# An RWKV-7 and Fourier-mixing kernel: who makes the decay totals, who turns r and v, and a new instruction order

**Chip, cores, metric.** One core of one Trainium2 chip. The time is the device time of one execution in microseconds (us); medians of several executions are given, with lowest and highest. A ratio is the mean time of one kernel's runs over the mean of the other kernel's runs in the same rounds, with a 95% interval, so it is not quite the ratio of the medians quoted beside it. Chips differ by one or two us, so kernels of different rounds are compared by their ratios to the kernel before.

## The reference

Inputs r, k, v, w, a, b have the shape 4 x 8 x 768 x 40 (batch, heads, time, head size), in float32.

```python
for t in range(S):                                   # RWKV-7 recurrence, per batch and head
    y[:, :, t] = einsum('bhd,bhde->bhe', rt, state)
    Sa = einsum('bhde,bhe->bhd', state, at)
    state = state * wt[:, :, None, :] - einsum('bhd,bhe->bhde', Sa, bt) + einsum('bhd,bhe->bhde', vt, kt)
x = y.transpose(0, 2, 1, 3).reshape(B, S, 320)
mixed = real(fft(fft(x, axis=1), axis=2))            # Fourier mixing over time and features
u = x + mixed
un = (u - mean(u)) / sqrt(var(u) + 1e-6)
out = u + maximum(un @ w_ch1, 0) @ w_ch2             # w_ch1 320 x 1280, w_ch2 1280 x 320
```

## The kernel before

The recurrence is computed in 24 chunks of 128 time steps, 6 to a batch. Each chunk is prepared (six loads of 160 KB, logarithms and cumulative sums of w, scaled and transposed inputs), then its chain updates the state, and after a batch's last chunk come the Fourier mixing and the feed-forward part (`post`). All engines run fixed lists: `ORDER` gives, for every operation, its place and its engine, and `SLOTS` the buffer that each intermediate takes. Every engine works through its list in order. `WARM` entries are matmuls on zeros that do nothing but fill TensorE's time.

The state update of a chunk needs the product of all its decays (the "total", `wt`). It is made in one of two ways:

```python
last, by_pe = c == NCH - 1, c < NCH - 1 and i not in WT_DMA
...
if by_pe:                                   # nine small matmuls in sums(), then one exponential
    op({"ACT": ... wt = exp(cum[:, DM:DM + 2 * NP])}, w=[wt], r=[cum], kind="wt")
...
if not last and not by_pe:                  # the last row of the sums, then a DMA that spreads it over partitions
    wt, row = buf(wt_s), new_row()          # the row pool has two buffers
    op({"ACT": ... row[96:] = exp(cum[96:, :DM]) ...}, w=[row], r=[cum], kind="row")
    op({"SP": (0.49, lambda: nc.sync.dma_start(
        wt().rearrange("p e q -> p (e q)"), row()[C - 1:C, :8 * C].rearrange("o (p j) -> o p j", j=8)))},
       w=[wt], r=[row], dma=0.2, kind="total")
```

The loads go by the same queue, SyncE's (`SP`), each as one `nc.sync.dma_start`. r and v are transposed either by one DMA transpose on that queue (`i in TURN_RV`) or by eight TensorE transposes and two evictions. The second weight matrix is loaded by `W2_PARTS` DMAs from GpSimd's queue.

## Time and profile before

| kernel before | |
|---|---|
| median of 4 runs beside the changed kernel | 234.84 us (233.29 to 235.43) |
| span of the profiled run, mean granted clock | 231.9 us, 1.00 |
| loads that landed before 46 us: median time from landing to first use | 0.4 us (of 44 loads; middle half 0.1 to 0.8) |
| last load of the first batch lands / that batch's last chunk ends its chain | 43.9 / 53.5 us |

How to read it: a median of 0.4 us between landing and first use says that the first 46 us are paced by the loads, whatever the engines do. From 72.6 us on TensorE paces it (the prediction shows the chain). Two rows of the page, in 40 slices of 5.8 us, the granted TensorE clock and the busy share of the DMA engines in tenths:

```profile
PEclk9999999999999999999999999999999999999999
DMA  6999999989998999969498999998974440000213
```

The first row has no dip; the second is at eight or nine up to slice 29 (168 us), but for slices 1, 18 and 20.

### The profile page before, as it was taken

The numbers are of one execution on the slowest core, as the hardware profiler recorded it, in microseconds if no ns is written. First come the engines' busy times: TensorE is split into PE (matmuls) and PEld (weight loads), VectorE is DVE, ScalarE is ACT, GpSimd is POOL, SyncE is SP. The second block draws the span as 40 slices with busy tenths as digits, with TensorE's granted clock in tenths as the row PEclk, the third lists the DMA queues.
The fourth block names the chain that finished last, engine by engine and source line by source line (L and its number), as shares of the span: only waits on it lengthen the run. The fifth ranks groups of instructions, "written<-read, shape, count | busy, mean of one in ns | idle before, by whom it ended". The sixth has DMA issues, their size and how long they took to land.

```text
span 231.9 us, 8953 instructions
## 1 busy us (share of the span) xinstructions
PE 223.8 (96%) x3617; PEld 171.0 (74%) x3617; DVE 206.0 (89%) x399; ACT 188.7 (81%) x381; POOL 153.9 (66%) x241
## 2 busy tenths in 40 slices
PE   7989999999999999999999999999999999999994
PEld 2557777878877777788877778878777777776573
DVE  6999999999999999889898988998999989589563
ACT  8999998989999998669999978998999886345300
POOL 7388978989998998442979968748965844200000
PEclk9999999999999999999999999999999999999999
DMA  6999999989998999969498999998974440000213
GB/s 120 189 159 190 167 159 161 173 140 176 159 196 153 164 189 178 170 130 162 88 218 149 182 158 176 169 170 130 230 137 76 83 105 31 3 0 0 88 57 113
DMA packets 165400, 31.88 MB, mean 137 GB/s; under 512 B 160560, under 2 KB 165040, under 8 KB 165360
## 3 DMA queue, kind: packets, MB, share of 16 engines
q1 hardware_dynamic: 163680, 29.69, 72.7%
q0 software_dynamic: 1680, 1.64, 4.6%
q8 instruction: 28, 0.46, 0.8%
q14 instruction: 12, 0.10, 0.1%
HBM read 26.87 MB, written 3.93 MB: 133 GB/s over the span
## 4 chain that ended last, share of the span: by engine, by line
PE 71%; DVE 10%; DMA 8%; POOL 4%; issue 3%; SPq 2%; ACT 2%; POOLq 0%; ACTq 0%; DVEq 0%
PE ps L167 71%; DMA in<-in_k_dram 4%; DVE pr L167 3%; POOL nat L167 2%; DMA in<-in_a_dram 2%; SPq L167 2%; DMA in<-in_w_dram 2%; DVE xb L167 2%; DVE m L167 1%; DVE xs L167 1%; DVE kb L167 1%; POOL pr L167 1%; ACT rw L167 1%; DVE sm L167 1%; DVE ar L167 0%
## 5 line engine op out<-in xcount | busy, mean ns | idle before, releaser
L167 PE MATMUL ps<-unT,w1sb 128*128 128x384 bf16 x240 | 46.7, 326 | 0.0
L167 POOL TENSOR_SCALAR_AFFINE_SELECT pr<-pr 128x1024 bf16<-128x1024 bf16 x32 | 34.8, 1096 | 16.3 <-ACT pr L167 16.3
L167 POOL TENSOR_TENSOR nat<-in,rw 128x320 bf16<-128x320 f32 x42 | 36.1, 866 | 7.7 <-DMA in<-in_k_dram 4.9
L167 PEld LDWEIGHTS <-nat 128*128 128x128 bf16 x576 | 34.0, 97 | 9.4 <-POOL nat L167 2.5
L167 PE MATMUL ps<-ident,nat 128*128 128x128 bf16 x416 | 36.3, 219 | 1.8 <-POOL nat L167 1.0
L167 ACT ACTIVATE pr<-ps 128x1024 bf16<-128x1024 f32 x33 | 33.6, 1032 | 3.4 <-PE ps L167 3.1
L167 PE MATMUL ps<-w2sb,h 128*128 128x320 bf16 (+1 forms) x250 | 35.7, 294 | 0.0
L167 PEld LDWEIGHTS <-pr 128*128 128x128 bf16 x768 | 28.9, 96 | 6.6 <-DVE pr L167 0.6
L167 ACT ACTIVATE h<-ps 128x384 bf16<-128x384 f32 x48 | 23.0, 494 | 8.3 <-PE ps L167 8.1
L167 PEld LDWEIGHTS <-h 128*128 128x128 bf16 x250 | 23.1, 98 | 8.2
L167 DVE TENSOR_TENSOR pr<-ps,su 128x1024 bf16<-128x1024 f32 x23 | 27.9, 1217 | 0.8 <-PE ps L167 0.4
L167 PEld LDWEIGHTS <-w1sb 128*128 128x128 bf16 x240 | 21.0, 97 | 10.2
L167 POOL TENSOR_TENSOR pm<-xb 128x161 bf16<-128x161 f32 x39 | 20.0, 527 | 8.2 <-DVE xb L167 8.0
L167 POOL TENSOR_TENSOR nat<-in,wp 128x320 bf16<-128x320 f32 x22 | 19.2, 874 | 4.4 <-ACT wp L167 1.7
L167 DVE TENSOR_TENSOR m<-ps,su 128x1024 bf16<-128x1024 f32 x15 | 18.3, 1217 | 1.9 <-PE ps L167 1.5
L167 DVE TENSOR_TENSOR pr<-ps,nsu 128x1024 bf16<-128x1024 f32 x16 | 19.4, 1213 | 0.6 <-PE ps L167 0.6
L167 DVE TENSOR_SCALAR h<-ps 128x384 bf16<-128x384 f32 x32 | 16.5, 548 | 3.4 <-PE ps L167 3.3
L167 DVE SCALAR_TENSOR_TENSOR xb<-ps,bst,xb 128x320 f32<-128x320 f32 (+1 forms) x25 | 13.0, 531 | 5.1 <-PE ps L167 5.0
L167 PE MATMUL ps<-xs,pr 128*128 128x40 bf16 x384 | 17.3, 180 | 0.3 <-DVE xs L167 0.2
L167 PE MATMUL ps<-nat,pr 128*128 128x40 bf16 x384 | 17.2, 180 | 0.2 <-DVE pr L167 0.2
L167 PE MATMUL ps<-ar,kb 64*128 64x128 bf16 x384 | 16.7, 217 | 0.3 <-DVE pr L167 0.2
L167 POOL TENSOR_TENSOR low<-logw 128x320 f16<-128x320 f32 x19 | 13.7, 722 | 2.0 <-ACT logw L167 1.5
(145 smaller groups left out, 554.3 us busy)
## 6 DMA issues: line engine op xcount, KB each, us to landing
in<-in_w_dram SPq DMA_DIRECT2D x24, 160.0 KB, 3.7
in<-in_r_dram SPq DMA_DIRECT2D x24, 160.0 KB, 3.7
in<-in_a_dram SPq DMA_DIRECT2D x24, 160.0 KB, 3.8
in<-in_v_dram SPq DMA_DIRECT2D x24, 160.0 KB, 3.9
in<-in_b_dram SPq DMA_DIRECT2D x24, 160.0 KB, 3.9
in<-in_k_dram SPq DMA_DIRECT2D x24, 160.0 KB, 4.1
out_dram<-xb SPq DMA_DIRECT2D x23, 160.0 KB, 1.9
w2sb<-in_moe_w_ch_dram POOLq DMA_DIRECT2D x2, 400.0 KB, 6.3
```

Source lines behind the costliest of these rows:

```text
L167: i = f(*args, **kwargs)
```

## The change

The intent: less small work for TensorE early (totals of chunks 3, 4, 6 and 7 by DMA), fewer DMA transposes in the middle (r and v of chunks 16, 17 and 18 back on TensorE), the second weights in smaller pieces, and an order and buffer assignment made anew for this.

```diff
-TURN_RV = {16, 17, 18, 19, 20, 21, 22, 23}
+TURN_RV = {19, 20, 21, 22, 23}
-WT_DMA = {8, 9, 10, 11, 12, 13, 14, 15, 16, 17, 18, 19, 20, 21, 22, 23}
+WT_DMA = {3, 4, 5, 6, 7, 8, 9, 10, 11, 12, 13, 14, 15, 16, 17, 18, 19, 20, 21, 22, 23}
-W2_PARTS = 2
+W2_PARTS = 5
-ORDER = ("AJAAHDALDAIAAUDAPDAEDATD ... (some 2,200 entries)
+ORDER = ("AHAAIDCGGAdSATGBASAJAAQG ... (some 2,200 entries, all new; 38 filling matmuls for 24)
-SLOTS = ("BCADABBCAABCBAB ...
+SLOTS = ("ABCDABCABABCABA ...
```

## The prediction

> **What bounds the kernel now.** I read the page first, then the chain of waits, then a table of stretches, then the timelines of TensorE and of SyncE's DMA queue. The chain tells which engine sets the end, and when that begins:
>
> ```profile
> PE 71%; DVE 10%; DMA 8%; POOL 4%; issue 3%; SPq 2%; ACT 2%; POOLq 0%; ACTq 0%; DVEq 0%
> ...
> 29.00 3.67 DMA in<-in_w_dram
> 32.66 4.68 DMA in<-in_a_dram
> ...
> 43.73 5.47 DMA in<-in_k_dram
> ...
> 72.64 26.55 PE ps L167 x427
> ...
> 101.33 59.34 PE ps L167 x989
> ...
> 163.04 65.82 PE ps L167 x867
> ```
>
> The columns are start, length and what. Up to about 50 us the chain goes through input loads (three pieces of 3.7 to 5.5 us are shown), from 50 to 72 us through VectorE, and from 72.6 us to the end almost only through TensorE: 26.55 + 59.34 + 65.82 = 151.7 of the last 159 us. So time taken from TensorE after 72 us is worth its full length, and time taken from it before 50 us is worth little, because there it waits for loads. The stretches say the same (busy us and count of each engine, granted clock, DMA share, GB/s):
>
> ```profile
> 0.00:24.00 24.00, 21.12 (x299) 13.13 (x300) 21.30 (x42) 22.92 (x50) 17.10 (x52) 1.00 0.99 165
> 24.00:48.00 24.00, 22.83 (x483) 18.32 (x480) 22.96 (x35) 22.33 (x48) 20.91 (x31) 1.00 0.95 163
> 72.00:120.00 48.00, 47.83 (x753) 37.01 (x752) 44.52 (x95) 41.97 (x83) 36.38 (x50) 1.00 0.89 157
> 120.00:168.00 48.00, 47.88 (x835) 38.04 (x828) 44.25 (x82) 43.29 (x87) 37.55 (x53) 1.00 1.06 173
> ```
>
> VectorE and ScalarE are at 90% or more beside TensorE, and the DMA share is about 1 until 168 us. The clock is 1.00 everywhere. A busy TensorE is not a full one, so I worked out from the starts of all 3617 matmuls in the trace how much room there is: 197.6 us of work at each form's own spacing, 4.6 us of filling matmuls that do nothing, and 25.2 us of gaps. 16.8 us of the gaps are before 72 us and 8.4 us after it, 5% of that part. The prices of what the change moves come from TensorE's timeline where chunk 7's totals are made:
>
> ```profile
> 42.61 0.16 PE L167 MATMUL ps<-ones,logw 128*128 128x2 bf16 x1
> 42.63 0.16 PE L167 MATMUL ps<-ones,low 128*128 128x2 bf16 x1
> ...
> 42.81 0.17 PE L167 MATMUL ps<-off_d,ident 128*128 128x8 bf16 x1
> 42.84 0.30 PE L167 MATMUL ps<-logw,ut 128*128 128x320 bf16 x1
> 42.97 0.30 PE L167 MATMUL ps<-low,ut 128*128 128x320 f16 x1
> 43.11 0.39 PE L167 MATMUL ps<-ident,nat 128*128 128x128 bf16 x4
> 43.33 0.31 PE L167 MATMUL ps<-sn,nat 128*128 128x80 bf16 x4
> ```
>
> Read the starts, not the lengths: the nine small matmuls of one total take 42.84 - 42.61 = 0.23 us, although each is shown as 0.16 us long; a group of four transposes takes 43.33 - 43.11 = 0.22 us.
>
> **What the Trainium skill says.** "TensorE: Matmul & The Clock Gate", section "Wait — 56ns, not 53.3ns?", gives the warm spacing as N / 2.4 GHz plus about 2.5 ns, and a floor of about 25 ns however small N is. The trace agrees: 55 ns for each transpose of 128 columns, 25 to 26 ns for each matmul of 2 columns. "Perfetto Trace Analysis", section "Tensor Engine Instruction (MATMUL, LD_WEIGHTS)", says that matmul ends are estimated; this is why I take starts. "DMA: Bandwidth & Descriptors", section "Anatomy of one DMA — SWDGE (gpsimd) path", says that a DMA's semaphore wait is held by the issuing sequencer before dispatch, so an early total whose row isn't ready would hold up the loads behind it. The trace has a mild form: SyncE's queue waited 2.2 us for ScalarE's rows in two places. The same page, "Specifications", gives 512 B as the least size for line rate; here 160560 of 165400 packets are smaller, and the loads bring 163 to 173 GB/s at a full share.
>
> **The change part by part.**
>
> *Totals.* A total is made by DMA from chunk 3 on instead of chunk 8; chunk 5 is the last of its batch and has none, so four chunks change (3, 4, 6, 7). TensorE loses 4 x 9 matmuls, 4 x 0.23 = 0.92 us. ScalarE loses 4 x 0.18 us (wt) and gains 4 x 0.43 us (row): +1.0 us. The queue gains four DMAs of 4 KB. These chunks are prepared between about 18 and 59 us, mostly where TensorE waits for loads anyway, so I count a good third of the 0.92: -0.35 us.
>
> *r and v.* Chunks 16, 17 and 18 go back to TensorE: 3 x 8 = 24 transposes, 6 groups of 0.22 = +1.33 us, between about 120 and 152 us, in the middle of the 59 us piece of the chain, so all of it counts. VectorE or ScalarE gets three more evictions of 512 columns (0.42 us on VectorE, 0.60 on ScalarE) and three that are 1024 wide instead of 512 (about +0.4 us each): some 2.6 us on two engines that have 8.5 us free between them from 120 to 168 us. It fits, with less slack. Three DMA transposes leave the queue (1.3 us to issue, 3.3 us to landing each). From 120 to 168 us the DMA is full, but TensorE has only some 3 us of gaps there, so I give that relief -0.3 us.
>
> *Second weights.* Two DMAs of 400 KB, 0.94 us each on GpSimd, become five of 160 KB, by the 0.66 us of a first-weight DMA about 3.3 us: +1.4 us on GpSimd, which is idle 34% of the span. They were issued at 80 and 82 us and first used after 94 us. Hidden: 0.
>
> *Order.* In the built order the last load of the first batch is DMA 38 of SyncE's queue (one of the 37 before it a total) and was DMA 42. At the measured pitch, 42 issues from 0.8 to 39.7 us or 0.95 us each, the batch is complete 3.8 us earlier, and the second half's work, which keeps TensorE full, can begin earlier. The price: chunks 6, 7 and 8 are complete 2, 4 and 5 places later (46 for 44, 53 for 49, 62 for 57). From 36 to 60 us the gaps were 4.9 of 24 us, 20%; 3.8 us of such time turned full is worth 0.2 x 3.8 = -0.8 us. The engine choices move too: counting forms in both built orders at the durations of the table of forms, VectorE loses about 1.5 us, ScalarE is even within 0.2, GpSimd gains about 6 us (six more folds, three more low parts, five weight DMAs). Slack goes to the engines that lack it; I give it -0.7 us of the 8.4 us of late gaps. The filling matmuls rise from 10,824 to 16,472 columns, 4.5 to 6.9 us at 2.4 GHz, all but a little in the first 25 us or so, where TensorE waits: 0, with a risk of half a microsecond.
>
> The sum: -0.35 + 1.33 - 0.3 - 0.8 - 0.7 = -0.8 us, so 234.6 - 0.8 = 233.8. The new order was presumably made for these settings and kept because it was good, so I take a little more off: **233.2 us**.
>
> **The rivals.**
> 1. *The late transposes decide.* TensorE is the bound from 120 to 168 us, the order's gains are small, and the time rises by the 1.33 us and some waits for the added evictions: 235.5 to 236.5. For it: the chain has nothing but TensorE there, with VectorE at 92%. Against it: the same order moves work off VectorE.
> 2. *Early totals become a wait.* When the DMA is full a total lands late: the eighth's was issued at 63.3 and landed at 69.7 us, and the state update that needs it began at 72.0. Chunk 4's total is now DMA 43; it would be issued at about 41 us, land at about 47, and chunk 4's update ran at 44.2 us before, so the state could come some 2.5 us late, and everything of chunk 5 behind it in TensorE's fixed order. If nothing else fills, this takes the 0.8 us back and costs 1 to 2 more: 235 to 237. Against it: the new order may have room just there, and a total isn't always so slow (median 2.6 us).
> 3. *The early part gains more.* The gaps before 72 us are 16.8 us, and loads at 38 instead of 42 may close 3 to 4 us of them, as TensorE is full once the first batch is complete: 230 to 231. Against it: no load has become cheaper, what comes earlier for one chunk comes later for the next, and the later chunks had only 0.6 to 3 us of slack.
>
> | step | effect on the end, us |
> |---|---|
> | totals | -0.35 |
> | r and v on TensorE | +1.33 |
> | DMA relief from 120 to 168 us | -0.3 |
> | weights in five | 0 |
> | first batch earlier | -0.8 |
> | later gaps | -0.7 |
>
> **Range and chances.** The 2% line is 4.7 us, at 229.9 and 239.3. The named terms are all under 1.4 us; only the order could move more, and it has 25 us of gaps to work on, of which I don't expect over 4 to go. The runs of before spread over 2.1 us. Eight times in ten I expect 229.8 to 236.4. Faster by over 2%: 0.11; within 2%: 0.84; slower by over 2%: 0.05.
>
> **What would show it.** Right: TensorE's matmuls on row totals fall from 28 + 28 + 7 to 12 + 12 + 3 and transposes of nat rise from 416 to 440; the chain goes into TensorE's long pieces a few us before 72.6; between 120 and 168 us TensorE stays as full as before with 24 more transposes. Rival 1 would show as more gaps of TensorE on VectorE and ScalarE evictions from 120 to 168 us. Rival 2 would show as a state update of chunk 3, 4, 6 or 7 that starts on a landing, "DMA wt<-row" in the chain. Rival 3 would show as 3 us or more fewer gaps before 72 us. I'm wrong in kind if the last load of a later batch, or a weight transfer, appears in the chain after 72 us.

## The result, and the profile after

| | before | changed |
|---|---|---|
| median (lowest to highest), 4 runs each | 234.84 us (233.29 to 235.43) | 240.61 us (240.19 to 241.99) |
| ratio | | 1.0266 (1.0201 to 1.0331): slower |
| span and clock of the profiled run | 231.9 us, 1.00 | 239.0 us, 0.993 |
| clock in the four runs | 1.00 in the profiled run | 0.993, 0.993, 0.993, 0.986 |
| median time from landing to first use, loads up to 46 us | 0.4 us | 2.3 us |
| last load of the first batch lands / its last chain ends | 43.9 / 53.5 us | 37.8 / 53.6 us |

Executions over 1.5% slower than the fastest of the same kernel are left out of the means. The prediction (233.2 us, 229.8 to 236.4) is wrong: the time lies 4.2 us above the range. The page of the changed kernel:

```profile
PEclk9999999999997999999999999999999999999999
DMA  7999998969999899989372798889478520002104
...
PE 73%; ACT 11%; DVE 6%; DMA 4%; issue 3%; POOL 2%; ACTq 0%; DVEq 0%; POOLq 0%
PE ps L168 73%; DMA wt<-row 4%; ACT pr L168 2%; DVE pr L168 1%; ACT h L168 1%; ACT wp L168 1%; ACT row L168 1%; POOL nat L168 1%; ACT logw L168 1%; DVE h L168 1%; ACT nat L168 1%; ACT kb L168 1%; ACT rw L168 1%; DVE xs L168 1%; POOL sm L168 1%
```

The share of input loads in the chain has gone (there were 8% of DMA, nearly all loads), and one other transfer has come: `wt<-row`, a total, with 4%. The clock has a dip in slice 13 (72 to 78 us). The chain of waits of the changed kernel, as start, length and what:

```profile
61.73 8.53 DMA wt<-row
70.82 0.95 PE ps L168 x19
72.31 10.79 PE ps L168 x175
...
86.25 33.64 PE ps L168 x509
119.91 23.93 PE ps L168 x426
```

and its waits from 58 to 98 us (engine, what it wrote, what it waited for: us, times, longest):

```profile
ACT row L168 <- DMA wt<-row: 3.1, 1, 3.1
PE ps L168 <- ACT row L168: 2.6, 1, 2.6
```

Which total? The one issued at 61.73 us is chunk 8's, which both kernels make by DMA. It takes 8.5 us to land. Chunk 10's row has the same of the two row buffers and waits for that, ScalarE waits with it, and TensorE waits for the PSUM bank that the row is read from. TensorE stands for 2.8 us from 68.0 us on, and from 72.61 to 76.02 us its clock is granted at 0.5. Stretches of both kernels (busy us and count of TensorE, its weight loads, VectorE, ScalarE and GpSimd, then granted clock, DMA share, GB/s), first before, then changed:

```profile
48.00:60.00 12.00, 11.53 (x242) 9.64 (x239) 11.59 (x16) 10.79 (x25) 11.07 (x18) 1.00 0.95 162
60.00:72.00 12.00, 11.77 (x225) 9.64 (x221) 11.86 (x28) 11.95 (x23) 11.20 (x18) 1.00 1.06 180
```

```profile
48.00:60.00 12.00, 11.94 (x242) 10.11 (x240) 11.89 (x19) 11.83 (x26) 11.85 (x17) 1.00 0.81 137
60.00:72.00 12.00, 9.16 (x163) 7.37 (x161) 9.18 (x22) 8.87 (x19) 8.74 (x13) 1.00 1.03 178
72.00:84.00 12.00, 11.90 (x195) 9.17 (x194) 10.80 (x25) 11.36 (x25) 10.28 (x16) 0.86 0.93 155
```

TensorE, VectorE, ScalarE and GpSimd fall to about 9 of 12 us between 60 and 72 us, while the DMA is full again; and just before, from 48 to 60 us, the DMA was at 0.81. So transfers that could have been made before 60 us were made after it. Why, the experiments have to say.

Busy time hides how full TensorE is, so I worked out real work, filling matmuls and gaps from the starts of all matmuls (each at its form's own spacing, the rest of the distance to the next start being gap, so what half clock costs is counted as gap; us):

| stretch | before: work, fill, gap | changed: work, fill, gap |
|---|---|---|
| 0 to 36 | 20.4, 4.4, 9.9 | 17.9, 6.5, 10.4 |
| 36 to 60 | 18.9, 0.1, 4.9 | 19.7, 0.3, 3.9 |
| 60 to 96 | 32.6, 0.0, 3.4 | 28.6, 0.2, 7.2 |
| 96 to 192 | 89.8, 0.0, 6.2 | 89.8, 0.0, 6.2 |
| 192 to the end | 35.8, 0.0, 0.8 | 42.1, 0.0, 1.5 |

The late middle, where 24 transposes came in, is exactly as full as before. 4.0 of the 6.3 us of work that the changed kernel still has to do after 192 us were lost between 60 and 96 us.

### The profile page after: what moved, and what is told of

It reads as the page before. It is cut to its first block, busy times and chain, and to the rows that moved or that the text cites.

```text
span 239.0 us, 8965 instructions
## 1 busy us (share of the span) xinstructions
PE 228.5 (96%) x3619; PEld 175.2 (73%) x3619; DVE 204.9 (86%) x398; ACT 189.2 (79%) x379; POOL 158.8 (66%) x249
## 4 chain that ended last, share of the span: by engine, by line
PE 73%; ACT 11%; DVE 6%; DMA 4%; issue 3%; POOL 2%; ACTq 0%; DVEq 0%; POOLq 0%
PE ps L168 73%; DMA wt<-row 4%; ACT pr L168 2%; DVE pr L168 1%; ACT h L168 1%; ACT wp L168 1%; ACT row L168 1%; POOL nat L168 1%; ACT logw L168 1%; DVE h L168 1%; ACT nat L168 1%; ACT kb L168 1%; ACT rw L168 1%; DVE xs L168 1%; POOL sm L168 1%
## 5 line engine op out<-in xcount | busy, mean ns | idle before, releaser
L168 PE MATMUL ps<-unT,w1sb 128*128 128x384 bf16 x240 | 47.2, 326 | 0.0
L168 POOL TENSOR_SCALAR_AFFINE_SELECT pr<-pr 128x1024 bf16<-128x1024 bf16 x31 | 33.7, 1093 | 16.7 <-ACT pr L168 16.5
L168 POOL TENSOR_TENSOR nat<-in,rw 128x320 bf16<-128x320 f32 x44 | 38.0, 871 | 4.9 <-ACT nat L168 2.8
L168 PEld LDWEIGHTS <-nat 128*128 128x128 bf16 x600 | 34.9, 98 | 8.1 <-POOL nat L168 1.8
L168 PE MATMUL ps<-ident,nat 128*128 128x128 bf16 x440 | 36.6, 219 | 1.0 <-ACT nat L168 0.3
L168 PEld LDWEIGHTS <-pr 128*128 128x128 bf16 x768 | 29.3, 96 | 8.4 <-issue 2.9
L168 PE MATMUL ps<-w2sb,h 128*128 128x320 bf16 (+1 forms) x250 | 35.2, 294 | 0.0
L168 ACT ACTIVATE pr<-ps 128x1024 bf16<-128x1024 f32 x32 | 32.5, 1024 | 1.3 <-PE ps L168 0.9
L168 DVE TENSOR_TENSOR pr<-ps,su 128x1024 bf16<-128x1024 f32 x25 | 30.3, 1219 | 2.2 <-PE ps L168 1.1
L168 ACT ACTIVATE h<-ps 128x384 bf16<-128x384 f32 x54 | 25.3, 495 | 5.4 <-PE ps L168 5.2
L168 PEld LDWEIGHTS <-h 128*128 128x128 bf16 x250 | 23.3, 98 | 8.4
L168 PEld LDWEIGHTS <-w1sb 128*128 128x128 bf16 x240 | 20.4, 97 | 10.4 <-DVE unT L168 0.2
L168 POOL TENSOR_TENSOR pm<-xb 128x161 bf16<-128x161 f32 x45 | 22.1, 509 | 6.6 <-DVE xb L168 6.5
L168 POOL TENSOR_TENSOR nat<-in,wp 128x320 bf16<-128x320 f32 x22 | 19.0, 865 | 3.3 <-ACT wp L168 2.3
L168 PE MATMUL ps<-nat,pr 128*128 128x40 bf16 x384 | 17.0, 180 | 2.6 <-ACT row L168 2.6
L168 DVE TENSOR_TENSOR pr<-ps,nsu 128x1024 bf16<-128x1024 f32 x15 | 18.2, 1216 | 1.3 <-PE ps L168 1.2
L168 DVE TENSOR_TENSOR m<-ps,su 128x1024 bf16<-128x1024 f32 x15 | 18.2, 1216 | 0.9 <-ACT h L168 0.8
L168 DVE SCALAR_TENSOR_TENSOR xb<-ps,bst,xb 128x320 f32<-128x320 f32 (+1 forms) x25 | 12.7, 530 | 7.1 <-PE ps L168 6.8
L168 POOL TENSOR_TENSOR low<-logw 128x320 f16<-128x320 f32 x22 | 15.8, 720 | 4.2 <-ACT logw L168 4.2
L168 PE MATMUL ps<-ar,kb 64*128 64x128 bf16 x384 | 17.9, 221 | 0.4
L168 PE MATMUL ps<-xs,pr 128*128 128x40 bf16 x384 | 17.3, 180 | 0.2
L168 DVE TENSOR_SCALAR h<-ps 128x384 bf16<-128x384 f32 x26 | 13.8, 547 | 2.3 <-PE ps L168 1.9
```

The costliest lines, as they stand in the source:

```text
L168: i = f(*args, **kwargs)
```

## The experiments

All are timed against the kernel before in the same rounds. All outputs are correct except where said.

Two tools serve throughout. Where two kernels have the same order, I pair the same matmuls of their traces and compare the starts; "behind" and "ahead" mean this. And each timed run has its mean clock: a stretch of 3.41 us at half clock in a span of 239 us makes 0.993, so the clock tells which of the timed runs had one.

| run | median us (before in its rounds) | ratio (95%) |
|---|---|---|
| changed kernel | 240.61 (234.84) | 1.0266 (1.0201 to 1.0331) |
| new_order_old_settings | 249.33 (235.85) | 1.0562 (1.0532 to 1.0592) |
| old_order_new_settings | 249.59 (235.85) | 1.0590 (1.0545 to 1.0635) |
| own_row_for_chunk_10 | 243.17 (235.85) | 1.0335 (1.0279 to 1.0391) |
| first_weights_after_total | 242.30 (235.85) | 1.0282 (1.0255 to 1.0309) |
| early_totals_on_tensore | 238.04 (234.46) | 1.0116 (1.0054 to 1.0179) |
| early_totals_on_scalar_queue | 241.54 (234.46) | 1.0278 (1.0216 to 1.0341) |
| all_totals_on_scalar_queue | 253.81 (234.46) | 1.0789 (1.0701 to 1.0876) |
| old_order_early_totals_only | 246.52 (234.46) | 1.0495 (1.0419 to 1.0571) |
| four_idle_transfers | 240.75 (235.30) | 1.0247 (1.0175 to 1.0318) |
| total_of_7_three_loads_later | 239.05 (235.30) | 1.0107 (1.0003 to 1.0211) |
| old_order_early_totals_later | 237.38 (235.30) | 1.0131 (1.0034 to 1.0229) |
| old_order_rv_on_tensore | 240.78 (235.30) | 1.0245 (1.0163 to 1.0327) |
| no_late_fills | 237.55 (235.44) | 1.0081 (1.0054 to 1.0108) |
| early_totals_on_gpsimd_queue | 242.80 (235.44) | 1.0314 (1.0281 to 1.0348) |
| twelve_fills_in_old_order | 237.97 (235.44) | 1.0117 (1.0089 to 1.0145) |
| old_order_totals_from_10 | 235.33 (235.44) | 0.9986 (0.9965 to 1.0008) |
| early_totals_on_tensore_again | 240.18 (237.63) | 1.0144 (1.0086 to 1.0202) |
| r_v_not_turned (wrong result) | 238.70 (237.63) | 1.0048 (1.0025 to 1.0070) |

### First round: order against settings, and the two things at 61 us

My first theory was that the order is to blame, and that the settings are worth their few tenths. The first run takes the new order with the three old settings, the second the old order with the new ones; what a setting adds or drops was placed by hand.

```diff
 # new_order_old_settings: new ORDER,       # old_order_new_settings: old ORDER,
-WT_DMA = {3 ...}; TURN_RV = {19 ...}       -WT_DMA = {8 ...}; TURN_RV = {16 ...}
+WT_DMA = {8 ...}; TURN_RV = {16 ...}       +WT_DMA = {3 ...}; TURN_RV = {19 ...}
```

> The new order with all three settings of before (totals on TensorE for chunks 3, 4, 6, 7; r and v of chunks 16 to 18 turned by DMA; second weights in two). Theory A (the order costs the time: a row of chunk 10 that waits for a total in flight at 67 to 70 us, and a slow start): it stays slow, 238 to 241 us, since chunk 8's total and chunk 10's row are there with either setting. Rival B (the three settings cost the time): back to 233 to 236 us.

> The old order with all three settings of after, each added or dropped operation put at the place of the one that it replaces (one more buffer for turned a and r; the index table shares the second weights' memory). Theory A: within 2 us of before, 233.5 to 237 us, by the sum of the prediction's small terms and some for the unplanned places. Rival B: 239 us or more.

Both lie near 249.5 us, outside what either theory said. They don't tell order from settings, as each breaks the fit of one to the other. The first loses its time from 120 to 168 us, where its hand-placed DMA transposes of r and v land late: its chain has `157.97 5.21 DMA rv<-nat` there. But from 60 to 96 us it does 32.1 us of TensorE work, nearly the 32.6 of before and far from the 28.6 of the changed kernel, in the same order. So in this trace the loss at 60 us is missing although the order is the new one, which hints at a setting. That was the first useful hint; the fifth round shows its limit. The second run loses its time before 60 us, and is taken up below.

The next two take on the chain's own account: the row buffer, and the three transfers of the first weights issued between 59.8 and 61.9 us.

```diff
 # own_row_for_chunk_10
-row = new_row()
+row = buf(h1_s, ...) if i == 10 else new_row()      # a buffer that is free then, zeroed on GpSimd
 # first_weights_after_total: in ORDER, on GpSimd
-weights 1, 2, 3 at 59.8, 61.3 and 61.9 us
+weights 1, 2, 3 after chunk 9's second cast (67 us)
```

> After, with a row buffer of its own for chunk 10's total (in a tile of h that is free then), so that its row need not wait for chunk 8's total to be read. Theory A: the 3.1 us wait of ScalarE at 67 us is gone, TensorE's gap of 2.6 us and the stretch at half clock after it too: 3 to 4.5 us faster than after, 236 to 237.5 us. Rival B: less than 1 us of difference.

> After, with the three first-weight DMAs issued some us later on GpSimd, so that chunk 8's total is in the queues before them. If crowding by those weights makes the total take 8.5 us (theory A1), it lands in 2.5 to 5 us, the wait of ScalarE shrinks to 0 to 1 us and the time falls by 2 to 4 us, to 236.5 to 238.5 us, unless the weights now come late for the first use. If the loads ahead of it make it slow (rival A2), it still takes over 6.5 us and the time falls by less than 1 us.

Both expectations of a gain in time fell: 243.2 and 242.3 us. But the row's wait is gone in both traces, and so is its cost: at 70 us the two runs are 2.1 and 3.0 us ahead of the changed kernel. Each loses more later, by something that its own edit put there. In own_row_for_chunk_10 the chain goes through a load of r for as long; then, between 85 and 90 us, the run loses 3.8 us to the landing of chunk 10's total, whose row now keeps a buffer of the feed-forward part, with a gap of 2.6 us and 3.4 us of half clock:

```profile
60.90 8.65 DMA in<-in_r_dram
...
81.28 4.26 DMA wt<-h
```

In first_weights_after_total chunk 8's total lands in 3.8 us instead of 8.5, as theory A1 said. But between 75 and 80 us TensorE waits for the weights themselves (`PE ps L168 <- DMA w1sb<-in_moe_w_ch_dram: 2.6, 2, 1.6`), and the clock is at 0.5 for 6.8 us: 5.3 us are lost. So the row buffer was only the last to wait in a backlog: around 61 us loads, weights and totals stand in one line, and taking one out of it brings the next to the front. The question became why the line is longer than before.

### Second round: the four early totals

Theory T: the four early totals take SyncE's time. Before chunk 7's total SyncE stood still for its row. The queue (`SPq`: the time at which SyncE issues) and ScalarE's row, both of the changed kernel:

```profile
47.91 1.20 SPq L168 DMA_DIRECT2D wt<-row  x1
49.16 0.59 SPq L168 DMA_DIRECT2D in<-in_r_dram  x1
51.06 0.48 SPq L168 DMA_DIRECT2D wt<-row  x1
52.04 0.37 SPq L168 DMA_DIRECT2D in<-in_b_dram  x1
```

```profile
50.60 0.43 ACT L168 ACTIVATE row<-ps 32x320 f32<-32x320 f32 x1
```

The row ends at 51.03, the total goes at 51.06; the load before was done with at 49.75. That is 1.3 us in which no load is issued, and each of the four totals takes a further 0.65 to 1.25 us until the next load.

```diff
 # early_totals_on_tensore
-WT_DMA = {3, 4, 5, 6, 7, 8, ...}
+WT_DMA = {8, ...}                        # ORDER: `row` -> `wt` on ScalarE, four `total` on SyncE dropped
 # early_totals_on_scalar_queue (all_totals_on_scalar_queue: the same for all seventeen)
-op({"SP": ... nc.sync.dma_start(wt, row)})
+op({"ACT": ... nc.scalar.dma_start(wt, row)})   # chunks 3, 4, 6, 7, directly after the row
 # old_order_early_totals_only: the kernel before, old ORDER
-WT_DMA = {8, ...}
+WT_DMA = {3, ...}                        # six entries of the order after where `wt` was
```

> The changed kernel, with the totals of chunks 3, 4, 6 and 7 alone taken back to TensorE (36 small matmuls, about 0.9 us of work), everything else as changed. Theory T (the four early totals hold SyncE's queue until their rows are ready, so the loads behind them come about 2 us late, chunk 8's total and chunk 9's last load are caught behind the first weights, and TensorE loses about 3 us and a half-clock stretch from 60 to 96 us): 237 to 238.8 us, DMA share from 36 to 60 us above 0.93 (0.91 and 0.81 with the change), chunk 8's total landed by 67 us instead of 70.3, no wait of chunk 10's row on it, no granted clock of 0.5 near 72 us. Rival (the new order itself makes the backlog, whoever makes the totals): 240 to 242 us and the row wait stays.

> The changed kernel, with the same four totals still made by DMA but issued from ScalarE's own queue directly after the row that ScalarE writes; SyncE's queue carries loads only until chunk 8. Theory T: SyncE no longer waits, so the gain of taking them back to TensorE comes here too: 236.5 to 238.8 us, less about 0.3 us for each issue on ScalarE that lies on its path. Rival (it is the transfers themselves or their landing that cost, not SyncE's waiting): 240 to 242 us.

> As the run before, but all seventeen totals from chunk 3 on go by ScalarE's queue. If a total's long landing (8.5 us for chunk 8) comes from standing behind loads in SyncE's queue, chunk 8's total lands within 4 us of its issue and the time falls to 235.5 to 238 us. If it comes from all 16 engines being busy, the total lands as late as before and the time is that of the run before within 1 us, or worse, as ScalarE has to issue seventeen DMAs (up to 0.6 us each).

> The kernel before with one part of the change: totals of chunks 3, 4, 6 and 7 by DMA from SyncE's queue, placed by hand; its order is otherwise the old one. In that order the loads of the first 46 us land 0.1 to 0.5 us before their use, so a queue that waits 1 to 2 us for a row four times over must cost more than in the new order. Theory T: 238 to 244 us, losses between 20 and 60 us. Rival (early totals are free, as the prediction had it, -0.35 us): 234 to 236 us.

Taking the four totals back to TensorE gives 238.04 us, as theory T had it, though TensorE has 36 matmuls more to do. The pairing of matmuls says where: the changed kernel is 0.2 us ahead of this run at 65 us, 3.0 us behind at 70, 4.0 at 75, and stays 3.8 us behind to the end. The whole difference between the two traces arises at this one place. The dip has gone, and the DMA works before 60 us:

```profile
48.00:60.00 12.00, 11.94 (x245) 10.11 (x246) 11.82 (x19) 11.36 (x26) 11.71 (x17) 1.00 0.94 162
60.00:72.00 12.00, 11.84 (x232) 9.77 (x230) 11.89 (x27) 11.90 (x25) 10.64 (x16) 1.00 1.01 172
```

In the old order the same four totals alone cost 12 us. There the loads are needed 0.4 us after they land, and the rows are ready late; SyncE's queue and ScalarE's row for chunk 6:

```profile
35.16 0.64 SPq L167 DMA_DIRECT2D in<-in_r_dram  x1
39.72 0.48 SPq L167 DMA_DIRECT2D wt<-row  x1
```

```profile
39.26 0.43 ACT L167 ACTIVATE row<-ps 32x320 f32<-32x320 f32 x1
```

SyncE issues nothing from 35.8 to 39.7 us. Before the four totals it stood still for 1.3, 3.0, 3.9 and 3.3 us, counted from the end of the transfer before, 11.5 in sum, against 12.1 us between the medians; the paired matmuls are 11.0 us behind at the end, 9.1 of it by 55 us. This also explains old_order_new_settings, which has the same four places.

The run with ScalarE's queue missed theory T's number (241.5 us), but its trace doesn't show the backlog: from 60 to 96 us TensorE does 32.1 us of work and the clock is 1.00. From 12 to 60 us it does 30.3 us instead of 34.7, because now ScalarE stands still:

```profile
40.13 0.43 ACT L168 ACTIVATE row<-ps 32x320 f32<-32x320 f32 x1
41.81 0.48 ACTq L168 DMA_DIRECT2D wt<-row  x1
42.40 0.44 ACT L168 ACTIVATE wp<-ps 128x320 f32<-128x320 f32 x1 [1.83 <-DVE snT L168]
```

From the end of the row at 40.56 to the next activation at 42.40 are 1.84 us, where the changed kernel goes straight on (row at 38.39, next at 38.84). I had counted 0.3 us. Most of it is not the issue. By the semaphore numbers in the trace each of these totals shares its completion semaphore with a load from SyncE's queue, and it was issued 0.07 to 0.14 us after that load had landed (here a load of a, at 41.74 us). For this ScalarE waited 0.70, 1.25 and 1.20 us at chunks 4, 6 and 7; at chunk 3, where the load was in time, the next activation began 0.61 us after the row's end. So the run brought a wait of its own and doesn't price the plain issue of a total on ScalarE above these 0.6 us. With all seventeen totals there it is 253.8 us. Chunk 8's total did land fast, 3.2 us after its issue, as the expectation had it, but ScalarE waits for loads in the same way at five of the first seven totals (up to 3.2 us), and no time was gained.

### Third round: waiting or issuing, and r and v in the old order

```diff
 # four_idle_transfers: early_totals_on_tensore, and at the four old places on SyncE
+nc.sync.dma_start(idle_t[:, x], fill16[...].to_broadcast([1, 128, 8]))   # nobody reads idle_t
 # total_of_7_three_loads_later: the changed kernel, on SyncE
-load, TOTAL of 7, load, load, load
+load, load, load, load, TOTAL of 7
 # old_order_early_totals_later: old_order_early_totals_only, the four totals 3, 6, 6, 6 loads further back
 # old_order_rv_on_tensore: the kernel before
-TURN_RV = {16, ...}
+TURN_RV = {19, ...}
```

> The changed kernel with the totals of chunks 3, 4, 6 and 7 on TensorE (238.0 us in the run before), plus four small DMAs on SyncE's queue at the places where the changed kernel has these totals: the same 128 packets of 32 bytes, from a constant, into memory that nobody reads, so nothing ever waits for a row or for their landing. Theory I (a total costs SyncE its issue, about 0.65 us each, and the loads behind are late by their sum): 2.6 us of queue come back as a loss of 2 to 3 us, 240 to 241 us, chunk 8's total issued after 61.3 us (60.3 without). Theory W (only waiting for a row that isn't ready costs; a small DMA is free): 237.7 to 238.7 us.

> The changed kernel with one move: chunk 7's total, for whose row SyncE waited 1.3 us (49.75 to 51.06; the row was ready at 51.03), is put behind the next three loads. Theory W (waiting costs): 237.2 to 239.4 us, chunk 8's total issued by 60.5 us instead of 61.7, no wait of chunk 10's row of over 1.5 us. Theory I alone (the issues cost, the wait doesn't): 240 to 241 us.

> The run of the old order with early totals by DMA (246.5 us), in which SyncE stood still for rows for 1.2, 3.1, 3.7 and 3.3 us, with these four totals put 3, 6, 6 and 6 loads further back in SyncE's queue, so that the rows are ready when it gets there. Theory W: nearly all of the 12 us comes back, 234 to 235.5 us. Theories W and I together: the waits come back and the issues (4 times 0.65 us, less 0.9 us of TensorE's work saved) stay, 235.5 to 238 us. Rival (early totals need their own order whatever the queue does): above 240 us.

> The kernel before with one part of the change: r and v of chunks 16, 17 and 18 turned on TensorE (24 more transposes), placed by hand (the ar pool has one more buffer, whose memory comes from letting the index table lie in that of the second weights). The prediction's term: +1.33 us of TensorE's work less 0.3 us of DMA relief, +1.0 us: 235 to 236.3 us in these rounds. Rival 1 (the evictions wait too): 236.5 to 238 us.

Four small transfers that wait for nothing and that nothing waits for bring 1.0116 back to 1.0247, nearly the 1.0266 of the changed kernel, and with them the same waits at 70 us:

```profile
ACT row L168 <- DMA wt<-row: 2.2, 1, 2.2
PE ps L168 <- ACT row L168: 2.1, 1, 2.1
```

So the dependence on a row or a state update isn't needed: four more issues on SyncE are enough. (That the 128 small packets burden the DMA engines instead isn't tested by itself; a load of 160 KB has some 1000, by its rows of 40 floats.) Against the repeated control below (1.0144) the difference is 1.0 point, and there the intervals overlap. Moving the one total that waited by three loads gives a ratio of 1.0107, but only two runs are in it (237.7 and 236.7 us); the other two, at 240.4 and 241.5 us, are as slow as four_idle_transfers on the same chip. So this relief helps in some executions, and it isn't shown to be enough. In the old order, putting the totals where their rows are ready brings 1.0495 down to 1.0131, as theories W and I together said (235.5 to 238).

The table shows what goes together in the one trace of each run (TensorE work in us; when chunk 8's total was issued and landed; TensorE's longest gap from 64 to 74 us; half clock), and how many of the timed runs had a stretch at half clock anywhere. The first three rows have the four transfers on SyncE, the others don't; some come from the later rounds:

| run | work 12 to 60 | work 60 to 96 | total of 8: issued, landed | gap | clock 0.5 near 72 | timed runs with half clock |
|---|---|---|---|---|---|---|
| changed kernel | 34.7 | 28.6 | 61.7, 70.3 | 2.8 | 3.4 us | 4 of 4 |
| four_idle_transfers | 34.9 | 29.6 | 63.2, 70.1 | 2.3 | 3.4 us | 3 of 4 |
| total_of_7_three_loads_later | 34.3 | 32.0 | 60.9, 68.2 | 0.7 | none | 1 of 4 |
| early_totals_on_tensore | 35.5 | 32.1 | 60.3, 65.8 | 0.3 | none | 0 of 4 |
| early_totals_on_tensore_again | 35.6 | 30.6 | 62.1, 69.2 | 2.1 | none | 3 of 6 |
| no_late_fills | 35.6 | 31.7 | 60.5, 68.0 | 1.1 | none | 2 of 4 |
| r_v_not_turned | 34.0 | 31.0 | 63.6, 70.4 | 1.6 | none | 7 of 22 |
| early_totals_on_scalar_queue | 30.3 | 32.1 | 59.8, 63.6 | 0.2 | none | 1 of 4 |
| early_totals_on_gpsimd_queue | 29.4 | 31.6 | 61.0, 64.6 | 0.4 | none (6.8 us at 51) | 4 of 4 |

The gap goes with the landing of chunk 8's total: landed by 66 us it is at most 0.4 us, from 68 us on 0.7 to 2.8 us. The four transfers at their early places on SyncE go with the longest gaps and with half clock in 7 of 8 timed runs, against 3 of 10 with the totals on TensorE. But they don't make the gap alone: it is there, shorter, in three traces without them.

r and v on TensorE in the old order cost 5 us instead of 1 (240.8): beyond both theories. Its profiled run has two half-clock stretches, 2.9 us of its delay come before 80 us, where its order is that of the kernel before, and the 24 transposes were placed by hand; I take no size from it.

### Fourth round: fills, a third queue, the price of TensorE's time, a step the other way

```diff
 # no_late_fills: early_totals_on_tensore without the last 16 of 38 WARM entries
 # early_totals_on_gpsimd_queue: the changed kernel, chunks 3, 4, 6, 7
-nc.sync.dma_start(wt, row)
+nc.gpsimd.dma_start(wt, row)
 # twelve_fills_in_old_order: the kernel before, 12 WARM entries of 256 columns more among chunks 16 to 18
 # old_order_totals_from_10: the kernel before
-WT_DMA = {8, 9, 10, ...}
+WT_DMA = {10, ...}
```

> The run with the early totals on TensorE (238.0 us), without the last 16 of its 38 filling matmuls (6616 columns, 2.8 us of TensorE at 2.4 GHz, all after about 14 us). Theory F (the longer fills of the new order hold up real work in the first 50 us and are part of what still separates it from the kernel before): 236.5 to 237.5 us, granted clock still 1.00. Rival (they lie in time in which TensorE waits anyway, as the prediction said): 237.5 to 238.7 us. If they are what keeps the clock up: a stretch of granted clock 0.5 before 60 us and 239 us or more.

> The changed kernel with the four early totals issued from GpSimd's queue at the places in the order that they have now, well after their rows. Theory of SyncE's queue: SyncE gets about 3.9 us back; GpSimd, 98% busy from 36 to 60 us, pays some 0.7 us for each issue (a weight transfer took it 0.66 us): 237 to 239.5 us, chunk 8's total issued before 61 us, no half clock near 72 us. Rival (any total by DMA this early costs, whoever issues it): 240 to 242 us, as from ScalarE's queue.

> The kernel before, with nothing changed but twelve filling matmuls of 256 columns (1.31 us at 2.4 GHz, as much TensorE work as the 24 transposes of r and v) spread among the work of chunks 16 to 18. The prediction's assumption, that all of TensorE's work counts there: +1.1 to +1.5 us, 235.9 to 236.5 us if before is at 234.8. Rival (the gaps of TensorE take it up): less than +0.5 us. Both leave the evictions out, which are then what is left of the 5 us that r and v on TensorE cost in the old order.

> The change undone further than before had it: the kernel before with the totals of chunks 8 and 9 taken back to TensorE too (by DMA from chunk 10 on). Theory of SyncE's queue (a total costs the loads behind it its issue, 0.65 us, and what it waits, while TensorE pays 0.23 us): 233.4 to 234.4 us against 234.8, chunk 10's row without a wait. Rival (at 63 to 70 us the loads have over 4 us of slack in the old order, so SyncE's time is free there): 234.8 to 235.6 us.

Without the late fills the ratio is 1.0081 against 1.0116, 0.8 us less for 2.8 us of fills taken out, but the intervals overlap. The traces say less: at 65 us this run is 0.3 us ahead of the one with the fills, and 0.1 us ahead of its repetition. That speaks for the rival. The clock stays at 1.00 in the profiled run; two of the four timed runs had a stretch at half clock.

GpSimd's queue is worse than SyncE's (242.8 us), for a third reason. GpSimd comes to chunk 6's total only at 52.0 us (SyncE: 47.9), and now the state update waits, the very wait that rival 2 of the prediction had named, with 6.8 us of half clock after it:

```profile
DVE st L168 <- DMA wt<-row: 2.8, 1, 2.8
PE ps L168 <- DVE st L168: 2.5, 1, 2.5
```

Twelve fills of 1.31 us in sum cost about 2.5 us between the medians (1.0117). In the profiled run TensorE's gaps from 120 to 192 us grow from 4.7 to 6.3 us beside them, and the work falls 3.1 us behind while the fills run; one of them waits 0.57 us until ScalarE has read its PSUM bank. The same trace is 2.4 us behind at 70 us already, long before the first fill at 143.5 us, after a gap of 2.2 us behind a late load of v. So the size is uncertain, but "less than 0.5 us" is out. And a gap of some 2 us near 70 us can come in the old order too.

old_order_totals_from_10 was meant to beat both kernels. It is the same as before (0.9986, interval 0.9965 to 1.0008), as its rival said: at 63 to 70 us the old order's loads have over 4 us to spare, and SyncE's time is free.

### Fifth round: r and v in the new order

```diff
 # r_v_not_turned: early_totals_on_tensore; wrong on purpose
-turns += [(AT, (2, 3), 2), (VT, (4,), 1)]
+turns += [(AT, (2,), 1)] if i in (16, 17, 18) else [(AT, (2, 3), 2), (VT, (4,), 1)]
```

> The run with the early totals on TensorE once more, as the control of the next one, in the same rounds: 237.2 to 238.6 us, ratio to before 1.008 to 1.016.

> The control without turning r and v of chunks 16, 17 and 18 at all (wrong on purpose: these chunks use what an earlier chunk left in the buffers): 24 transposes, 1.33 us of TensorE, three evictions fewer and three half as wide. This is the prediction's term for r and v, measured in the new order without any placing by hand. As predicted (TensorE's length counts once, the evictions lie beside): 1.0 to 1.6 us below the control (0.4 to 0.7%). Rival from the twelve fills (it counts twice, with the waits it brings): 2.2 to 3.2 us below. Rival (gaps take it up): less than 0.6 us.

This chip was slower for all kernels. The control is at 1.0144, the kernel without these transposes at 1.0048: 0.96 points, 2.3 us of 237; the means, over all rounds, differ by 1.0 us (239.67 and 238.63). But these differences hold all that the two kernels lose before 75 us, by more or less luck. The traces separate it: from 75 us to the end the kernel without the transposes gains 0.5 us on the first run of the control, 0.7 on the second, 0.5 on no_late_fills and 0.5 on the changed kernel. So in the profiled runs the 1.33 us of transposes cost 0.5 to 0.7 us, and gaps took up the rest, nearly as the last rival had it.

The repeated control also limits the finding of the second round. Its profiled run has early totals on TensorE, and yet the wait at 70 us:

```profile
ACT row L168 <- DMA wt<-row: 2.0, 1, 2.0
PE ps L168 <- ACT row L168: 2.0, 1, 2.0
```

It is 1.8 us behind the first run of the same kernel at 70 us, and level with it before. In three of its six timed runs the mean clock is 0.991 to 0.993, in the four runs of the first time it was 0.998 to 1.00, and in the changed kernel it is 0.993 or less in all four. The chip has a part in this: in the rounds of the repetition the kernel before had such a clock in 6 of 27 runs, in those of the second round in none of 7.

## Why the prediction was wrong, point by point

**What bounds the kernel: right.** TensorE is the bound after 72 us in both traces, and what was lost by 75 us came through at full length: 4.0 us behind early_totals_on_tensore at 75 us, 3.8 at the end. Two readings were loose: in the lines shown VectorE is at 89 to 96% and ScalarE at 87 to 96%, not all at 90% or more, and the DMA is not full throughout until 168 us (0.76 from 96 to 120 us).

**Totals, -0.35 us: this is the step that failed.** The matmul counts came out as said (12 + 12 + 3), 36 fewer, which is TensorE's 0.9 us. But the working put "four DMAs of 4 KB" into the queue at no price. By the ratios, early totals through SyncE cost 1.2 to 1.5 points, 2.9 to 3.5 us, after TensorE's saving; by the paired matmuls 2.2 to 3.8 us, all between 65 and 75 us. What the traces show in a row is: four issues and one wait on SyncE, loads issued 1.2 to 2.2 us later from 52 to 61 us (one 3.3), the DMA at 0.81 before 60 us and full after, chunk 8's total landing at 70.3 us instead of 65.8 and 69.2, a gap of 2.8 us on TensorE instead of 0.3 and 2.1, and 3.4 us of half clock. The idle transfers show that the issues alone do it, with no data waited for. Why chunk 8's total lands 3.4 us apart in two executions of one kernel stays open; so the early totals are shown to lengthen this wait, and not to be its only cause.

**Rival 2** was nearest in kind, and I had quoted the sentence that leads there: the queue's wait holds the loads behind. But I looked for the harm at the state updates of chunks 3, 4, 6 and 7. These had time (chunk 3's total landed at 26.0 us for an update at 38.4, chunk 7's at 53.0 for one at 64.8). The harm came 10 us later, at a total that both kernels make by DMA. Only the GpSimd run showed the form that I had drawn.

**r and v, +1.33 us, less 0.3 us for the DMA: right in kind, rather too large.** The gaps from 96 to 192 us did not grow (6.2 us in both), so rival 1's sign is missing. The price in the traces of the new order is 0.5 to 0.7 us; not "all of it counts", as TensorE's gaps there took up about half. Nothing shows the 0.3 us of relief by itself.

**Second weights, 0: held as far as the trace goes.** TensorE never waits for them in it; no run tests this part alone.

**Order, -0.8 and -0.7 us: failed as well.** The first batch's loads did land earlier, by 6.1 us instead of the 3.8 expected. But its last chain ended at 53.6 us for 53.5. The loads had been the pace and no longer were: their time to first use rose from 0.4 to 2.3 us, and ScalarE's share of the chain rose from 2% to 11%. Taking one bound away let the next one, just behind it, set the same time. The gaps before 72 us, which rival 3 saw shrink by 3 us, grew from 16.8 to 18.5 us, and those after 72 us became 10.6 us from 8.4 and not fewer (the half clock is part of this).

**Fills, 0 with a risk of half a microsecond: held.** 0.1 to 0.3 us in the traces; the 0.8 us between the ratios are not settled.

By ratios the changed kernel is 6.2 us slower. The early totals (about 3), r and v (about 0.6) and the fills (about 0.2) make up some 4 of it. The other 2 us are left for the new order itself, which was to gain 1.5: that is what remains when the others are taken off, no run shows it alone, and both mixed runs broke too much to tell. No version tried is faster than the kernel before; the best of the new order stays 0.8% behind it.

## What to carry to other kernels

Price a small DMA by the time of the queue that issues it and by what stands behind it in that queue, not by its bytes; where a wait can't be avoided, put the transfer behind the loads that don't need it. One trace is one execution: the same kernel had a gap of 0.3 us in one and 2.1 us in another, so count over the timed runs too, and compare traces stretch by stretch before a size is taken from whole times. When a change moves something in a busy queue, look for the harm not only where the moved data is used but at the next place at which several transfers meet. When a profile says "loads bound this part", ask how far behind the next bound is before counting a gain from earlier loads.

## What the Trainium skill lacked or had wrong

- "DMA: Bandwidth & Descriptors", section "Issuing engines are not separate DMA queues", calls the time that a sequencer needs to initiate a DMA "usually small relative to the DMA itself". It doesn't say what this time does to the loads behind it in the queue: here four idle transfers of 4 KB, which took SyncE 0.6 to 2.5 us each to issue and 2.8 to 4.3 us to land, took a kernel from 1.0116 to 1.0247 of the time before.
- The same section says that starting DMAs on several engines saves sequencer time; it doesn't say what it costs the engine that takes them over. Here ScalarE's next activation began 0.6 us after the row when it issued a DMA of that row, and 1.3 to 1.8 us after it where the DMA's semaphore was still held by a load from SyncE's queue; the kernel did not gain (1.0278 for 1.0266).
- "TensorE: Matmul & The Clock Gate", section "Why this matters for your kernels", advises no gaps of TensorE above about 3 us. Here shorter ones were followed by a granted clock of 0.5 for 3.41 us: a gap of 2.3 us in four_idle_transfers, 2.8 us in the changed kernel; while one of 2.1 us in early_totals_on_tensore_again, one of 2.2 us in twelve_fills_in_old_order and one of 2.8 us in old_order_early_totals_only (at 30 us) were not. So the length of one gap doesn't decide it here. The length of the half-clock stretch does agree with the page's window of 3413 ns.
- No page has it that TensorE work put by hand into a full stretch can cost more than its length: 1.31 us of filling matmuls put the work 3.1 us behind, while 1.33 us of transposes that the order had been made for cost 0.5 to 0.7 us.
